# One pair of heads in a fused attention and two-layer network: another order of transposes, scores and products

## The chip, the cores and the metric

The kernel runs on one core of one Trainium2 chip. The metric is the device time of one execution in microseconds (us), as the median of several runs. An engine takes its instructions strictly in the order in which the program lists them; the engines meet only where one waits for a result of another. The names are those of the profile: PE is the matrix engine (PEld its weight loads), DVE the vector engine, ACT the scalar engine, SP the engine that issues most transfers.

## The reference

```python
scores = scale * np.matmul(q, k.transpose(0, 1, 3, 2))      # 2 batches, 12 heads, 448 x 64
scores = np.where(mask, -1000000000.0, scores)              # causal
scores = scores - np.max(scores, axis=-1, keepdims=True)
attn = np.exp(scores)
attn = attn / (np.sum(attn, axis=-1, keepdims=True) + 1e-09)
x = np.matmul(attn, v)                                      # then (896, 768)
h = np.maximum(x @ w_in, 0.0);  x = h * h @ w_out           # d_ff = 2048
h = x @ w_in2;                  out = (h - np.tanh(h)) @ w_out2
```

## The kernel before, in words

Two heads make a pair; there are twelve pairs, six for each batch (`NPAIR`, line 28). The 448 queries of a head are seven chunks of 64, and since the mask is causal chunk c needs keys 0 to 64(c+1)-1. A pair's work is cut into parts, each a function of `body`:

- `scores(n, t)` (lines 262 to 284), PE: the scores of half t of the pair's chunks, in two banks of PSUM. Half 0 is chunks 6, 5 and 0, half 1 is chunks 3, 2, 4 and 1 (`STEPS`, line 51; the first pair swaps them). Two small matmuls per bank add the mask (line 281). The banks of tag "s" are four, so a half's banks are those of the same half of the pair before.
- `maxes(n, t)` (lines 286 to 294), DVE: one maximum per chunk (line 292), and one scaling of the row of maxima (line 294).
- `exps(n, t, z)` (line 301), ACT: the exponentials with their sums.
- `recips(n)` (lines 305, 306), DVE: one over the sums. `norms(n, cs)` (line 313), DVE: the division, one instruction per chunk, in place, of 64(c+1) columns.
- `transposes(n, t)` (lines 315 to 322), PE: four of the sixteen 128x128 blocks of the probabilities into one bank of tag "t" (two such banks), and then on ACT the copy out to SBUF (line 322). Block group 0 reads chunks 0 to 3, group 1 chunks 4, 5, 6 and 2, groups 2 and 3 chunks 3 to 6.
- `pv(n, kcs)` (line 334), PE: the products with V, for key blocks 0 to 3. Key block 0 needs the copies of groups 0 and 1, block 1 that of group 2, blocks 2 and 3 that of group 3.
- `xhi` and `xlo` (lines 347, 351): the pair's output as a rounded high part (ACT) and a remainder (DVE).

The loop of lines 463 to 503 runs over s, and works on three pairs at once: the scores of pair s, the softmax of pair p = s-1, and transposes and products of pair a = s-2. No scheduler moves anything: an engine's queue is the order in which the loop's calls list its instructions.

Beside it the loop prepares the weights of the network. `one()` (lines 168 to 172) takes one DVE step of that list (`shift`, `merge`, `sign`, `split`, lines 113 to 134) if the step's budget allows, which is about one step per pair. The ACT work that belongs to it (lines 103 and 125) is kept in `act_late` and issued where `late()` (line 164) is called.

After the loop, lines 505 to 538 finish the last two pairs between the first matmul groups of the network (`first`, line 422, `group`, lines 357 to 367), and lines 540 to 555 run the network. Its matmuls have the lines 364, 365 and 366.

Of the kernel before, what the change touches and what calls it, by code (L numbers as in the profile page):

```python
# [8 lines left out]
F32 = mybir.dt.float32  # L9
# [13 lines left out]
P = 128  # L23
# [39 lines left out]
def body(ctx: ExitStack, tc: tile.TileContext, qT, kT, vL, w1, w2, w3, w4, out):  # L63
    nc = tc.nc
    sb = ctx.enter_context(tc.tile_pool(name="sb", bufs=1))
    ps = ctx.enter_context(tc.tile_pool(name="ps", bufs=1, space=PSUM))
# [7 lines left out]
    def slot(i, shape, dt, name):  # L74
        return sb.tile(shape, dt, tag=f"slot{i}", name=name)
# [75 lines left out]
    def room():  # L151
        i = len(taken) - RING
        return i < 0 or taken[i] < freed[0]
# [10 lines left out]
    def late():  # L164
        while act_late:
            act_late.pop(0)()

    def one():

        if todo and budget[0] > 0 and (room() or not todo[0][3]):  # L170
            take()
            return True

    def take():
        f, cost, _, _ = todo.pop(0)
        f()
        budget[0] -= cost
# [19 lines left out]
    def load_qk(n):  # L197
        if n < NPAIR:
            b, hp = divmod(n, NP)
            qk[n] = (tmp(f"q{n}"), tmp(f"k{n}", "w"))  # L200
            nc.sync.dma_start(out=qk[n][0], in_=qT[b, hp])
            (nc.scalar if n == 0 else nc.sync).dma_start(out=qk[n][1], in_=kT[b, hp])

    def load_v(b):
        t = sb.tile([P, 3, DM], F32, tag=f"v{b}", name=f"v{b}")
        nc.sync.dma_start(out=t, in_=vL[b, : 3 * P].rearrange("(t p) d -> p t d", p=P))
        if b == 0:
            vs["end"] = slot(7, [D, B, DM], F32, "vend")
            nc.sync.dma_start(out=vs["end"], in_=vL[:, 3 * P :].rearrange("b p d -> p b d"))
        vs[b] = [t[:, 0], t[:, 1], t[:, 2], vs["end"][:, b]]  # L210
# [5 lines left out]
    def warm(count):  # L216
        o = ps.tile([P, 512], F32, tag="o", bufs=2, name="warm")[:, :S]
        for _ in range(count):
            nc.tensor.matmul(o, lhsT=ones[:, :P], rhs=ones, start=True, stop=True)  # L219
# [33 lines left out]
    sc = {}  # L253
    stat = {}
    pt = {}
    ob = {}

    def step(n, t):

        return STEPS[1 - t if n == 0 else t]  # L260

    def scores(n, t):
        q, k = qk[n]
        banks = []
        for z, cs in enumerate(step(n, t)):
            bank = ps.tile([P, 512], F32, tag="s", bufs=4, name=f"s{n}_{t}_{z}")
            banks.append(bank)
            for c in cs:
                sc[n, c] = bank[:, SOFF[c] : SOFF[c] + D * (c + 1)]
        for i in range(2):  # L270
            for z, cs in enumerate(step(n, t)):
                for c in cs[i : i + 1]:
                    for j in range(2):
                        r, e = slice(D * j, D * j + D), D * (j ^ z)
                        nc.tensor.matmul(sc[n, c][e : e + D], lhsT=q[r, D * c : D * c + D], rhs=k[r, : D * (c + 1)], start=(c == cs[0]), stop=False, skip_group_check=True)  # L275
        for z, cs in enumerate(step(n, t)):
            d = [SOFF[c] // D + c for c in cs]
            o = banks[z].rearrange("p (b k) -> p b k", k=D)[:, d[0] : d[-1] + 1 : max(d[-1] - d[0], 1)]
            for j in range(2):
                r, e = slice(D * j, D * j + D), D * (j ^ z)  # L280
                nc.tensor.matmul(o[e : e + D], lhsT=identb[r, r], rhs=maskb[r, : len(cs)], start=False, stop=True, skip_group_check=True)
        if t == 1:
            qk.pop(n)
            load_qk(n + 3)

    def maxes(n, t):
        if t == 0:
            stat[n] = sb.tile([P, 3, 8], F32, tag="stat", bufs=3, name=f"st{n}")
        st = stat[n]
        cs = [c for b in step(n, t) for c in b]  # L290
        for c in cs:
            nc.vector.tensor_reduce(out=st[:, 0, SI[c] : SI[c] + 1], in_=sc[n, c], axis=AX.X, op=ALU.max, negate=True)  # L292
        a, z = SI[cs[0]], SI[cs[-1]] + 1
        nc.vector.tensor_scalar_mul(out=st[:, 0, a:z], in0=st[:, 0, a:z], scalar1=0.125)  # L294

    def exps(n, t, z):
        st = stat[n]
        for c in step(n, t)[z]:
            w = D * (c + 1)
            i = SI[c]  # L300
            nc.scalar.activation(prob[n % 3][:, POFF[c] : POFF[c] + w], sc.pop((n, c)), AF.Exp, bias=st[:, 0, i : i + 1], scale=0.125, accum_out=st[:, 1, i : i + 1])  # L301

    def recips(n):
        st = stat[n]
        nc.vector.tensor_scalar_add(out=st[:, 1, :NQ], in0=st[:, 1, :NQ], scalar1=1e-9)
        nc.vector.reciprocal(out=st[:, 2, :NQ], in_=st[:, 1, :NQ])

    def norms(n, cs):
        st = stat[n]
        for c in cs:  # L310
            i = SI[c]
            p = prob[n % 3][:, POFF[c] : POFF[c] + D * (c + 1)]
            nc.vector.tensor_scalar_mul(out=p, in0=p, scalar1=st[:, 2, i : i + 1])  # L313

    def transposes(n, t):
        if t == 0:
            pt[n] = slot(3 + n % 2, [P, 16, P], F32, f"pt{n}")
        bank = ps.tile([P, 512], F32, tag="t", bufs=2, name=f"t{n}_{t}")
        for i, (kc, c) in enumerate(TBLK[4 * t : 4 * t + 4]):
            o = bank.rearrange("p (i j q) -> p i j q", j=2, q=D)[:, i, :: -1 if c in TURNED else 1]  # L320
            nc.tensor.transpose(o, prob[n % 3][:, POFF[c] + P * kc : POFF[c] + P * kc + P], ident)  # L321
        nc.scalar.copy(out=pt[n][:, 4 * t : 4 * t + 4], in_=bank.rearrange("p (i q) -> p i q", q=P))  # L322

    def pv(n, kcs):
        b, hp = divmod(n, NP)
        if 0 in kcs:
            ob[n] = ps.tile([P, 512], F32, tag="o", bufs=2, name=f"o{n}")
        o = ob[n]
        for kc in kcs:
            r = P if kc < 3 else D  # L330
            m = NQ - 2 * kc
            for j in range(2):
                h = 2 * hp + j
                nc.tensor.matmul(  # L334
                    o[D * j : D * j + D, P * kc : S],
                    lhsT=vs[b][kc][:r, D * h : D * h + D],
                    rhs=pt[n][:r, TBASE[kc] : TBASE[kc] + m, D * j : D * j + D],
                    start=(kc == 0),
                    stop=(kc == 3),
                    skip_group_check=True,  # L340
                )
        if 3 in kcs:
            pt.pop(n)

    def xhi(n):
        b, hp = divmod(n, NP)
        nc.scalar.copy(out=x[hp][:, 0, b], in_=ob[n][:, :S])  # L347

    def xlo(n):
        b, hp = divmod(n, NP)  # L350
        nc.vector.tensor_sub(out=x[hp][:, 1, b], in0=ob.pop(n)[:, :S], in1=x[hp][:, 0, b])
# [111 lines left out]
    for s in range(NPAIR):  # L463
        p, a = s - 1, s - 2
        sp, sa = p >= 0, a >= 0
        budget[0] = min(budget[0], 0) + (SHARE_PAIR if s > 1 else 0)
        if sa:
            transposes(a, 0)
        if sp:
            maxes(p, 1)  # L470
            exps(p, 1, 0)
        if sa:
            transposes(a, 1)
        if sp:
            exps(p, 1, 1)
        one()
        if a >= 1:
            xhi(a - 1)
        scores(s, 0)
        maxes(s, 0)  # L480
        if sp:
            recips(p)
            norms(p, (3, 2))
        if s == 2:
            warm(5)
        if a >= 1:
            xlo(a - 1)
        if sa:
            transposes(a, 2)
            transposes(a, 3)  # L490
        exps(s, 0, 0)
        exps(s, 0, 1)
        if sp:
            norms(p, (1, 0, 4, 5, 6))
        if sa:
            pv(a, (0, 1))
        late()
        scores(s, 1)
        one()
        if sa:  # L500
            pv(a, (2, 3))
        if s == 1:
            load_v(1)

    p, a = NPAIR - 1, NPAIR - 2
    budget[0] = min(budget[0], 0) + SHARE_LAST
    transposes(a, 0)
    maxes(p, 1)
    exps(p, 1, 0)
    transposes(a, 1)  # L510
    exps(p, 1, 1)
    one()
    xhi(a - 1)
    act = first(0, 0, 0, 0)
    recips(p)
    norms(p, (3, 2))
    xlo(a - 1)
    transposes(a, 2)
    transposes(a, 3)
    act()  # L520
    norms(p, (1, 0, 4, 5, 6))
    act = first(0, 0, 1, 0)
    pv(a, range(4))
    late()
# [5 lines left out]
    act = first(0, 0, 2, 0)  # L530
    for t in range(4):
        transposes(p, t)
    act()
    pv(p, range(4))
    late()
# [57 lines left out]
```

## Time and profile before

| | |
|---|---|
| median of 3 runs | 568.91 us (567.93 to 569.95) |
| profiled execution, its own time | 567.94 us |
| span of the profiled execution | 566.2 us |
| PE busy | 553.8 us, 98% of the span |
| DVE busy | 405.6 us, 72% |
| ACT busy | 336.8 us, 59% |
| PE, DVE, ACT busy from 37.04 to 78.53 us (six pairs) | 39.68, 38.26, 36.47 of 41.49 us |
| first matmul of the network (line 364) | 85.25 us after the span's start |

The span goes from the first to the last instruction; the execution's own time has 1.7 us more around it. The shares of the whole span are means over two stages: some 85 us of attention, in which three engines hand work to each other, and 480 us of network, in which PE works without a break.

### The profile page before, as it was taken

To read this page: it belongs to the slowest core of one execution; us is meant where nothing else is said; L and a number is where in the kernel's file an instruction comes from. 1 tells how busy PE (TensorE), PEld (TensorE's weight loads), DVE (VectorE), ACT (ScalarE), POOL (GpSimd) and SP (SyncE) were. 2 spreads that over 40 slices of the span, in tenths; PEclk is the share of its full clock that TensorE was granted. 3 is DMA by queue.
4 is the path that set the end of the run, shared out by engine and by line. 5 is a ranking of instruction groups with operands and counts; after the bars stand their busy time and mean duration, and the time that the engine had idled before them with its cause. 6 is when DMAs were issued, how large, how long until landed. Compare 5 with 4: busy or idle time off the path is not lost.

```text
span 566.2 us, 8063 instructions
## 1 busy us (share of the span) xinstructions
PE 553.8 (98%) x3134; PEld 479.5 (85%) x3134; DVE 405.6 (72%) x727; ACT 336.8 (59%) x650; POOL 1.8 (0%) x11
## 2 busy tenths in 40 slices
PE   6899999999999999999999999999999999999997
PEld 3455558899999999999999999999999999999996
DVE  5889995588667527665648579998887499898511
ACT  4798896777654336666424258786565487864100
POOL 1000000000000000000000000000000000000000
PEclk9999999999999999999999999999999999999999
DMA  8732301245355514333133330110665311015211
GB/s 279 296 123 66 107 1 57 59 164 167 113 168 167 168 56 168 111 112 111 57 112 112 111 113 1 56 56 11 214 218 172 118 50 56 1 57 184 81 49 49
DMA packets 15525, 61.85 MB, mean 109 GB/s; under 512 B 1664, under 2 KB 6400, under 8 KB 15488
## 3 DMA queue, kind: packets, MB, share of 16 engines
q1 hardware_dynamic: 15200, 61.00, 32.5%
q8 instruction: 24, 0.39, 0.3%
q10 hardware_dynamic: 288, 0.34, 0.2%
q14 instruction: 13, 0.11, 0.1%
HBM read 58.59 MB, written 2.75 MB: 108 GB/s over the span
## 4 chain that ended last, share of the span: by engine, by line
PE 90%; ACT 8%; DVE 2%; issue 0%; DVEq 0%; ACTq 0%
PE o L364 14%; PE o L365 14%; PE h L364 14%; PE o L366 14%; PE h L366 14%; PE h L365 14%; ACT p L301 4%; ACT pt L322 3%; PE o L334 3%; PE s L275 2%; PE t L321 1%; DVE st L292 1%; PE warm L219 1%; ACT x L347 1%; DVE p L313 0%
## 5 line engine op out<-in xcount | busy, mean ns | idle before, releaser
L364 PE MATMUL o<-g,w 128*128 128x448 f32 x384 | 141.3, 368 | 0.0
L365 PE MATMUL o<-g,w 128*128 128x448 f32 x384 | 141.2, 368 | 0.0
L366 PE MATMUL o<-g,w 128*128 128x448 f32 x384 | 140.3, 365 | 0.0
L364 PEld LDWEIGHTS o<-g,w 128*128 128x128 f32 x384 | 71.9, 187 | 7.2
L366 PEld LDWEIGHTS o<-g,w 128*128 128x128 f32 x384 | 72.1, 188 | 6.9
L125 ACT CAST w<-raw 128x768 fp32r<-128x768 f32 x64 | 57.9, 904 | 33.3 <-DVE raw L123 33.2
L365 PEld LDWEIGHTS o<-g,w 128*128 128x128 f32 x384 | 72.1, 188 | 6.4
L103 ACT ACTIVATE raw<-raw 128x768 f32<-128x768 f32 x64 | 59.3, 926 | 23.9 <-DMA raw<-w 23.9
L364 PE MATMUL h<-y,w 128*128 128x448 f32 x192 | 70.5, 367 | 0.0
L364 PE MATMUL h<-x,w 128*128 128x448 f32 x192 | 70.4, 367 | 0.0
L366 PE MATMUL h<-x,w 128*128 128x448 f32 x192 | 70.0, 365 | 0.0
L366 PE MATMUL h<-y,w 128*128 128x448 f32 x192 | 69.7, 363 | 0.0
L365 PE MATMUL h<-x,w 128*128 128x448 f32 x192 | 69.5, 362 | 0.0
L365 PE MATMUL h<-y,w 128*128 128x448 f32 x192 | 69.3, 361 | 0.0
L123 DVE SCALAR_TENSOR_TENSOR raw<-raw 128x768 int32<-128x768 int32 x64 | 61.2, 956 | 1.3
L118 DVE SCALAR_TENSOR_TENSOR raw<-raw 128x768 int32<-128x768 int32 x64 | 61.0, 953 | 0.9 <-ACT raw L103 0.9
L134 DVE TENSOR_TENSOR w<-raw,w 128x768 fp32r<-128x768 f32 x32 | 30.6, 958 | 28.0 <-ACT w L125 27.9
L373 DVE TENSOR_TENSOR g<-r,g 128x448 fp32r<-128x448 f32 x32 | 20.0, 625 | 37.8 <-ACT g L370 37.8
L301 ACT ACTIVATE p<-s,st 128x256 f32<-128x256 f32 (+6 forms) x84 | 40.1, 511 | 8.1 <-DVE st L294 7.0
L132 DVE SCALAR_TENSOR_TENSOR w<-w,raw 128x768 fp32r<-128x768 f32 x32 | 30.7, 959 | 18.7 <-ACT w L125 18.5
L366 PEld LDWEIGHTS h<-y,w 128*128 128x128 f32 x192 | 35.9, 187 | 3.5
L366 PEld LDWEIGHTS h<-x,w 128*128 128x128 f32 x192 | 36.0, 187 | 3.0
(57 smaller groups left out, 742.7 us busy)
## 6 DMA issues: line engine op xcount, KB each, us to landing
raw<-w SPq DMA_DIRECT2D x64, 768.0 KB, 4.3
q<-qT SPq DMA_DIRECT2D x12, 224.0 KB, 4.6
k<-kT SPq DMA_DIRECT2D x11, 224.0 KB, 3.1
out<-part SPq DMA_DIRECT2D x11, 224.0 KB, 1.9
v<-vL SPq DMA_DIRECT2D x2, 1152.0 KB, 10.1
vend<-vL SPq DMA_DIRECT2D x1, 384.0 KB, 10.0
k<-kT ACTq DMA_DIRECT2D x1, 224.0 KB, 3.5
out<-part ACTq DMA_DIRECT2D x1, 112.0 KB, 1.7
```

The costliest lines, as they stand in the source:

```text
L103: nc.scalar.activation(h, h, AF.Copy, scale=2.0**-112)
L118: nc.vector.scalar_tensor_tensor(out=lo, in0=hi, scalar=3, in1=lo, op0=ALU.logical_shift_left, op1=ALU.bitwise_or)
L123: nc.vector.scalar_tensor_tensor(out=lo, in0=hi, scalar=-0x80000000, in1=lo, op0=ALU.bitwise_and, op1=ALU.bitwise_or)
L125: act_late.append(lambda: nc.scalar.copy(out=st["w"][:, 0], in_=lo.bitcast(F32)))
L132: nc.vector.scalar_tensor_tensor(out=w[:, 1], in0=w[:, 0].bitcast(F32), scalar=-(1.0 - 2.0**-24), in1=f, op0=ALU.mult, op1=ALU.add)
L134: nc.vector.tensor_sub(out=w[:, 1], in0=f, in1=w[:, 0])
L301: nc.scalar.activation(prob[n % 3][:, POFF[c] : POFF[c] + w], sc.pop((n, c)), AF.Exp, bias=st[:, 0, i : i + 1], scale=0.125, accum_out=st[ ...
L322: nc.scalar.copy(out=pt[n][:, 4 * t : 4 * t + 4], in_=bank.rearrange("p (i q) -> p i q", q=P))
L364: nc.tensor.matmul(h, lhsT=hi, rhs=xh, start=(k == 0), stop=False)
L365: nc.tensor.matmul(h, lhsT=hi, rhs=xl, start=False, stop=False)
L366: nc.tensor.matmul(h, lhsT=lo, rhs=xh, start=False, stop=(k == kk - 1))
L373: nc.vector.tensor_sub(out=dst[1], in0=v, in1=dst[0])
```

## The change

The copies leave `transposes` and become a function of their own, `tcopy`. Within a step the order becomes: transposes of groups 0 and 1, scores of half 0, transposes of groups 2 and 3, scores of half 1, and then all products with V in one run. On ACT both exponentials of half 1 come first and the copies of groups 0 and 1 behind them, and `late()` stands ahead of the exponentials of half 0. On DVE the divisions are cut elsewhere: chunks 1, 0, 2 and 3 stay in the step of the sums, chunks 4, 5 and 6 go to the next step, behind the maxima of half 1. No instruction is added or left out.

```diff
--- before.py
+++ after.py
@@ -253,6 +253,7 @@
     sc = {}
     stat = {}
     pt = {}
+    tb = {}
     ob = {}
 
     def step(n, t):
@@ -313,12 +314,15 @@
             nc.vector.tensor_scalar_mul(out=p, in0=p, scalar1=st[:, 2, i : i + 1])
 
     def transposes(n, t):
-        if t == 0:
-            pt[n] = slot(3 + n % 2, [P, 16, P], F32, f"pt{n}")
-        bank = ps.tile([P, 512], F32, tag="t", bufs=2, name=f"t{n}_{t}")
+        bank = tb[n, t] = ps.tile([P, 512], F32, tag="t", bufs=2, name=f"t{n}_{t}")
         for i, (kc, c) in enumerate(TBLK[4 * t : 4 * t + 4]):
             o = bank.rearrange("p (i j q) -> p i j q", j=2, q=D)[:, i, :: -1 if c in TURNED else 1]
             nc.tensor.transpose(o, prob[n % 3][:, POFF[c] + P * kc : POFF[c] + P * kc + P], ident)
+
+    def tcopy(n, t):
+        if t == 0:
+            pt[n] = slot(3 + n % 2, [P, 16, P], F32, f"pt{n}")
+        bank = tb.pop((n, t))
         nc.scalar.copy(out=pt[n][:, 4 * t : 4 * t + 4], in_=bank.rearrange("p (i q) -> p i q", q=P))
 
     def pv(n, kcs):
@@ -464,61 +468,67 @@
         p, a = s - 1, s - 2
         sp, sa = p >= 0, a >= 0
         budget[0] = min(budget[0], 0) + (SHARE_PAIR if s > 1 else 0)
-        if sa:
-            transposes(a, 0)
         if sp:
             maxes(p, 1)
-            exps(p, 1, 0)
         if sa:
+            norms(a, (4, 5, 6))
+            transposes(a, 0)
             transposes(a, 1)
         if sp:
+            exps(p, 1, 0)
             exps(p, 1, 1)
+        if sa:
+            tcopy(a, 0)
+            tcopy(a, 1)
         one()
         if a >= 1:
             xhi(a - 1)
         scores(s, 0)
         maxes(s, 0)
+        if s == 2:
+            warm(5)
         if sp:
             recips(p)
-            norms(p, (3, 2))
-        if s == 2:
-            warm(5)
+        if sa:
+            transposes(a, 2)
+            tcopy(a, 2)
+            transposes(a, 3)
+            tcopy(a, 3)
+        if sp:
+            norms(p, (1, 0, 2, 3))
+        late()
+        exps(s, 0, 0)
+        exps(s, 0, 1)
         if a >= 1:
             xlo(a - 1)
+        one()
+        scores(s, 1)
         if sa:
-            transposes(a, 2)
-            transposes(a, 3)
-        exps(s, 0, 0)
-        exps(s, 0, 1)
-        if sp:
-            norms(p, (1, 0, 4, 5, 6))
-        if sa:
-            pv(a, (0, 1))
-        late()
-        scores(s, 1)
-        one()
-        if sa:
-            pv(a, (2, 3))
+            pv(a, range(4))
         if s == 1:
             load_v(1)
 
     p, a = NPAIR - 1, NPAIR - 2
     budget[0] = min(budget[0], 0) + SHARE_LAST
+    maxes(p, 1)
+    norms(a, (4, 5, 6))
     transposes(a, 0)
-    maxes(p, 1)
+    transposes(a, 1)
     exps(p, 1, 0)
-    transposes(a, 1)
     exps(p, 1, 1)
+    tcopy(a, 0)
+    tcopy(a, 1)
     one()
     xhi(a - 1)
     act = first(0, 0, 0, 0)
     recips(p)
-    norms(p, (3, 2))
     xlo(a - 1)
     transposes(a, 2)
+    tcopy(a, 2)
     transposes(a, 3)
+    tcopy(a, 3)
     act()
-    norms(p, (1, 0, 4, 5, 6))
+    norms(p, (1, 0, 2, 3, 4, 5, 6))
     act = first(0, 0, 1, 0)
     pv(a, range(4))
     late()
@@ -530,6 +540,7 @@
     act = first(0, 0, 2, 0)
     for t in range(4):
         transposes(p, t)
+        tcopy(p, t)
     act()
     pv(p, range(4))
     late()
```

DVE, in step 4 of the loop and into step 5; s is a bank of scores, st the row of statistics of a pair, p the probabilities of a pair, x its output, o its products. Before:

```order
L351 TENSOR_TENSOR x_68<-o_403,x_68 128x448 [waits Activation_49]
L313 TENSOR_SCALAR p_126<-p_126,st_373 128x128
L313 TENSOR_SCALAR p_126<-p_126,st_373 128x64
L313 TENSOR_SCALAR p_126<-p_126,st_373 128x320
L313 TENSOR_SCALAR p_126<-p_126,st_373 128x384
L313 TENSOR_SCALAR p_126<-p_126,st_373 128x448
L292 TENSOR_REDUCE st_468<-s_1_0_503 128x1 [waits PE_49]
L292 TENSOR_REDUCE st_468<-s_1_0_503 128x1
L292 TENSOR_REDUCE st_468<-s_1_1_504 128x1 [waits PE_49]
L292 TENSOR_REDUCE st_468<-s_1_1_504 128x1
L294 TENSOR_SCALAR st_468<-st_468 128x4 [waits DVE_49]
L134 TENSOR_TENSOR w_359<-raw_120,w_359 128x768
```

The same place now (line numbers are higher by one to four):

```order
L314 TENSOR_SCALAR p_126<-p_126,st_373 128x192
L314 TENSOR_SCALAR p_126<-p_126,st_373 128x256
L355 TENSOR_TENSOR x_68<-o_420,x_68 128x448 [waits Activation_49]
L293 TENSOR_REDUCE st_468<-s_1_0_495 128x1 [waits PE_49]
L293 TENSOR_REDUCE st_468<-s_1_0_495 128x1
L293 TENSOR_REDUCE st_468<-s_1_1_496 128x1 [waits PE_49]
L293 TENSOR_REDUCE st_468<-s_1_1_496 128x1
L295 TENSOR_SCALAR st_468<-st_468 128x4 [waits DVE_49]
L314 TENSOR_SCALAR p_126<-p_126,st_373 128x320
L314 TENSOR_SCALAR p_126<-p_126,st_373 128x384
L314 TENSOR_SCALAR p_126<-p_126,st_373 128x448
L134 TENSOR_TENSOR w_359<-raw_120,w_359 128x768
```

The divisions of 320, 384 and 448 columns of a pair stood ahead of the maxima of the other pair's half 1; now they stand behind these maxima and their scaling, and ahead of the step of weight preparation.

PE, the end of step 4; t is a bank of transposes, pt their copies, v the values. Before:

```order
L334 MATMUL o_498<-pt_432,v_112 64x448 x2
L334 MATMUL o_498<-pt_432,v_112 64x320 [waits Activation_49]
L334 MATMUL o_498<-pt_432,v_112 64x320
L275 MATMUL s_1_0_503<-k_232,q_231 64x256 x2
L275 MATMUL s_1_1_504<-k_232,q_231 64x320 x2
L275 MATMUL s_1_0_503<-k_232,q_231 64x192 x2
L275 MATMUL s_1_1_504<-k_232,q_231 64x128 x2
L281 LDWEIGHTS identb
L281 MATMUL s_1_0_503<-maskb,identb 64x2x64
L281 LDWEIGHTS identb
L281 MATMUL s_1_0_503<-maskb,identb 64x2x64
```

Now:

```order
L282 LDWEIGHTS identb
L282 MATMUL s_1_1_496<-maskb,identb 64x2x64
L282 LDWEIGHTS identb
L282 MATMUL s_1_1_496<-maskb,identb 64x2x64
L338 MATMUL o_513<-pt_451,v_112 64x448 x2
L338 MATMUL o_513<-pt_451,v_112 64x320 [waits Activation_49]
L338 MATMUL o_513<-pt_451,v_112 64x320
L338 MATMUL o_513<-pt_451,v_112 64x192 [waits Activation_49]
L338 MATMUL o_513<-pt_451,v_112 64x192
L338 MATMUL o_513<-pt_451,vend 64x64 x2
L320 MATMUL t_0_530<-ident,p_126 128x2x64 [waits DVE_49,PE_49]
```

The scores of half 1 stood between the products of key blocks 1 and 2, and so behind two waits for copies; now all products stand behind these scores, and ahead of the next transposes.

ACT, step 5. Before:

```order
L301 ACTIVATE p_127,st_468<-s_0_0_456,st_468 128x448 [waits DVE_49]
L301 ACTIVATE p_127,st_468<-s_0_1_457,st_468 128x384
L301 ACTIVATE p_127,st_468<-s_0_1_457,st_468 128x64
L322 COPY pt_525<-t_0_526 128x512 [waits PE_49,Activation_49]
L301 ACTIVATE p_127,st_468<-s_1_0_503,st_468 128x256 [waits DVE_49]
L301 ACTIVATE p_127,st_468<-s_1_0_503,st_468 128x192
L322 COPY pt_525<-t_1_539 128x512 [waits PE_49]
L301 ACTIVATE p_127,st_468<-s_1_1_504,st_468 128x320
L301 ACTIVATE p_127,st_468<-s_1_1_504,st_468 128x128
L347 CAST x_69<-o_498 128x448
L322 COPY pt_525<-t_2_573 128x512 [waits PE_49]
L322 COPY pt_525<-t_3_579 128x512 [waits PE_49]
```

Now:

```order
L302 ACTIVATE p_127,st_468<-s_0_0_456,st_468 128x448 [waits DVE_49]
L302 ACTIVATE p_127,st_468<-s_0_1_457,st_468 128x384
L302 ACTIVATE p_127,st_468<-s_0_1_457,st_468 128x64
L302 ACTIVATE p_127,st_468<-s_1_0_495,st_468 128x256 [waits DVE_49,PE_49]
L302 ACTIVATE p_127,st_468<-s_1_0_495,st_468 128x192
L302 ACTIVATE p_127,st_468<-s_1_1_496,st_468 128x320 [waits PE_49]
L302 ACTIVATE p_127,st_468<-s_1_1_496,st_468 128x128
L326 COPY pt_544<-t_0_530 128x512 [waits PE_49,Activation_49]
L326 COPY pt_544<-t_1_535 128x512 [waits PE_49]
L351 CAST x_69<-o_513 128x448
L326 COPY pt_544<-t_2_570 128x512 [waits PE_49]
L326 COPY pt_544<-t_3_576 128x512 [waits PE_49]
```

The copies of groups 0 and 1 stood ahead of and between the exponentials of half 1 (256, 192, 320 and 128 columns), and now stand behind all four.

## Rows read from the trace of the kernel before

**Rows 1.** One period by stretch: from:to, us, busy PE PEld DVE ACT POOL, clock, DMA.
```profile
50.87:57.79 6.92, 6.62 (x69) 3.77 (x69) 6.44 (x21) 6.47 (x21) 0.00 (x0) 1.00 0.23 66
```
**Rows 2.** Chain that ended last, over one period: start us, us, what.
```profile
43.68 0.59 ACT pt L322
...
47.45 0.76 PE o L334 x4
...
49.92 0.60 PE t L321 x4
...
50.60 0.59 ACT pt L322
```
**Rows 3.** Timeline of DVE, one period: start us, us, engine, line, operation [idle before].
```profile
49.33 1.27 DVE L292 TENSOR_REDUCE st<-s 128x1 f32<-128x256 f32 x4
50.64 0.17 DVE L294 TENSOR_SCALAR st<-st 128x4 f32<-128x4 f32 x1
50.72 0.95 DVE L123 SCALAR_TENSOR_TENSOR raw<-raw 128x768 int32<-128x768 int32 x1
51.97 1.22 DVE L292 TENSOR_REDUCE st<-s 128x1 f32<-128x448 f32 x3 [0.30 <-PE s L281]
53.23 0.17 DVE L294 TENSOR_SCALAR st<-st 128x3 f32<-128x3 f32 x1
53.44 0.17 DVE L305 TENSOR_SCALAR st<-st 128x7 f32<-128x7 f32 x1
53.64 0.20 DVE L306 RECIPROCAL st<-st 128x7 f32<-128x7 f32 x1
53.88 0.58 DVE L313 TENSOR_SCALAR p<-p,st 128x256 f32<-128x256 f32 x2
54.38 0.62 DVE L351 TENSOR_TENSOR x<-o,x 128x448 fp32r<-128x448 f32 x1
54.91 1.43 DVE L313 TENSOR_SCALAR p<-p,st 128x128 f32<-128x128 f32 x5
56.25 0.42 DVE L292 TENSOR_REDUCE st<-s 128x1 f32<-128x256 f32 x1
```
**Rows 4.** Groups by line and form, DVE, 36.98 to 78.5 us: the divisions moved.
```profile
L313 DVE TENSOR_SCALAR p<-p,st 128x448 f32<-128x448 f32 x6 | 2.7, 447 | 0.0
...
L313 DVE TENSOR_SCALAR p<-p,st 128x384 f32<-128x384 f32 x6 | 2.5, 413 | 0.0
L313 DVE TENSOR_SCALAR p<-p,st 128x320 f32<-128x320 f32 x6 | 2.3, 379 | 0.0
```
**Rows 5.** Timelines of DVE, PEld and PE: where scores wait for divisions, and maxima for scores.
```profile
11.86 1.93 DVE L313 TENSOR_SCALAR p<-p,st 128x256 f32<-128x256 f32 x7
...
13.84 0.20 PEld L321 LDWEIGHTS t<-ident,p 128*128 128x128 f32 x2 [0.23 <-DVE p L313]
14.21 0.21 PEld L275 LDWEIGHTS s<-k,q 64*64 64x64 f32 x8 [0.17 <-ACT pt L322]
...
50.87 0.99 PE L275 MATMUL s<-k,q 64*64 64x448 f32 x12
```
**Rows 6.** Timelines of PEld, ACT and DVE in the step of pair 2.
```profile
15.19 0.69 PEld L219 LDWEIGHTS <-const-bfloat16-1.0 128*128 128x128 bf16 x5
...
17.40 1.09 ACT L322 COPY pt<-t 128x512 f32<-128x512 f32 x2
...
19.81 0.96 ACT L103 ACTIVATE raw<-raw 128x768 f32<-128x768 f32 x1
...
20.80 0.96 DVE L118 SCALAR_TENSOR_TENSOR raw<-raw 128x768 int32<-128x768 int32 x1 [0.86 <-ACT raw L103]
21.68 0.42 DVE L292 TENSOR_REDUCE st<-s 128x1 f32<-128x256 f32 x1
```
**Rows 7.** Timeline of PEld at the end of attention: last transposes, first matmul of the network.
```profile
84.42 0.86 PEld L321 LDWEIGHTS t<-ident,p 128*128 128x128 f32 x8
85.25 0.19 PEld L364 LDWEIGHTS h<-x,w 128*128 128x128 f32 x1
```

## The prediction

> **What bounds the kernel now.** I read the views in this order: busy time by stretch, the chain that ended last, then the timelines of single engines. From the first matmul of the network on, at 85.25 us [rows 7], PE works without a break and the change touches nothing, so what counts is by how much that matmul moves. It stands at the end of a regular stretch: one pair every 6.92 us, at a granted clock of 1.00, which is the 2.4 GHz level, with PE busy for 6.62 of it, DVE for 6.44 and ACT for 6.47 [rows 1]. In that table the reader is to see that three engines are nearly full, so none has much to give. The chain over one period says what closes the loop today: it runs through copies and exponentials on ACT, then through products, scores and transposes on PE, and back to the next copy 6.92 us later [rows 2]. DVE is not on it, but waits only 0.30 us for scores in each period [rows 3].
>
> The change takes PE out of ACT's way: the products no longer wait for the copies of groups 2 and 3 ahead of the scores of half 1. The question is which loop is the longest after it. The new order on DVE makes one: transposes of group 1 read chunks 4, 5 and 6; the divisions of these now stand behind the maxima of half 1 of the next pair; the scores of half 0 stand on PE behind those transposes; and the maxima of half 0 wait on DVE for these scores. DVE does nothing else in that wait but one step of weight preparation.
>
> **The loop through DVE, link by link.** I start the count at the first maximum of half 1 and use distances from start to start.
>
> 1. Four maxima: 49.33 to 50.64, 1.31. Their scaling: the next independent instruction starts 0.08 later [rows 3].
> 2. Divisions of chunks 4, 5 and 6: 0.379, 0.413 and 0.447 long [rows 4]. Five such divisions run from 54.91 to 56.34, while the next instruction starts at 56.25 [rows 3], so neighbours overlap by 0.09; I take 0.08. The three end 0.30 + 0.33 + 0.447 = 1.08 after the first starts.
> 3. Seven divisions end at 13.79 and the transposes that waited for them start at 13.84: 0.05. Those are the last two of group 1, just the two that will stand behind chunk 6's division, and the scores start at 14.21: 0.37 [rows 5].
> 4. Scores start at 50.87 [rows 5], the maxima of half 0, which waited for them, at 51.97: 1.10 [rows 3].
> 5. Maxima of half 0: 51.97 to 53.23, 1.26. Scaling 0.08, as in link 1. The sums are ready by then (ACT's exponentials of half 1 start right after link 1), so today's longer gap to 53.44 goes. One over the sums: 53.44 to 53.64 to 53.88, 0.44 [rows 3].
> 6. Divisions of chunks 1, 0, 2 and 3: all seven take 53.88 to 54.38 and 54.91 to 56.25, 1.84 [rows 3]; less 0.30 + 0.33 + 0.36 for the three of link 2 leaves 0.85. Then the remainder of the output, 54.38 to 54.91: 0.53. Then the next maxima.
>
> Links 1 to 3 are 1.31 + 0.08 + 1.08 + 0.05 + 0.37 = 2.89; the whole loop is 2.89 + 1.10 + 1.26 + 0.08 + 0.44 + 0.85 + 0.53 = **7.15 us, against 6.92 now**: 0.23 more for each pair. Between divisions and maxima of half 0, DVE has 3.99 - 2.38 = 1.61 us, of which the weight step takes 0.95 [rows 3]; some 0.66 us are a wait that takes the place of 0.30 today.
>
> The other engines fit into 7.15. PE's 6.62 hold waits that now fall away, and ACT's 6.47 contain a weight step [rows 1]. On PE the scores of half 1 follow about 2 us after those of half 0 and so are there more than 1 us before DVE comes to them; the products stand in the time in which PE would wait for the divisions anyway. On ACT the copies wait for nothing that is late. `late()`, now ahead of the exponentials of half 0, puts one weight step ahead of them; they are not needed before the sums of the next step. SP issues the same transfers in the same order, each behind the scores it followed before. So what the change saves on PE (a run of products without a change of kind in its middle, no wait for copies) is covered by the wait for DVE, and costs or gives nothing.
>
> **The start.** The divisions of pair 0 begin at 11.86 as now [rows 5]. Four of them (0.85) instead of seven stand ahead of the maxima of pair 1's half 1, which start at 12.71. By links 1 to 3 the scores of pair 2 start at 15.60 (14.21 now [rows 5]), and by links 4 to 6 DVE is through with the divisions of pair 1 at 15.60 + 1.10 + 1.26 + 0.08 + 0.44 + 0.85 = 19.33. In this step a second weight step follows (line 118), which waits for ACT's line 103. ACT does it behind the copies of groups 2 and 3: scores about 0.97, five warming matmuls about 0.75 [rows 6], transposes and 0.70 to the copy (49.92 to 50.60 in the chain [rows 2]), two copies with 0.94 to the next instruction (1.09 long [rows 6], less an overlap of 0.15 as among ACT's neighbours), so it starts at 18.96, ends 0.96 later [rows 6], and line 118 starts at 19.95 and holds DVE for 0.88 (20.80 to 21.68 [rows 6]). The maxima of pair 2's half 1 start at about 20.83.
>
> **The sum.** Nine loops of 7.15 us bring the maxima of pair 11's half 1 to 20.83 + 64.35 = 85.18. The network's first matmul takes the place of the next scores: 2.89 later, less 0.17, because the eight transposes ahead of it take 0.83 to its start [rows 7] and there is no gap of 0.17 as there is to the scores [rows 5]. That is 87.90, against 85.25: **+2.65 us**. The profiled execution would go from 567.94 to 570.6 us. It lies 0.97 us under the median of the runs, 568.91; I forecast for the median: **571.6 us**. The tail behind it keeps its length, since PE is full there and the copies of pairs 10 and 11 have a whole matmul group of the network to land in.
>
> Bounds: a hundredth of a microsecond in the loop is a tenth in the sum. Links 3 and 4 are each one crossing of engines, read from one or two places; 0.06 either way is 0.6 us. The start is between 20.21 for the maxima (line 118 waits for nothing: 19.33 + 0.88) and 21.5 (a copy or a transfer late): -0.6 to +0.7. Together +1.3 to +4.0 us.
>
> A page to weigh against link 2: five divisions that sum to more than 1.7 us start and hand over within 1.34 [rows 3], so neighbours on DVE overlap. The Trainium skill, VectorE: DVE Perf Modes, section The DRAIN you can't avoid, says that the next operation does not start until the pipe is empty, though one that is not held starts earlier. With full durations everywhere the loop would come to some 8 us and the sum to over 10 us more; the trace decides for the overlap.
>
> **Rivals.**
>
> *Faster: DVE's loop does not close.* Were the three divisions done before PE reaches group 1, DVE would run through without the wait and need its busy 6.44 us [rows 1] for a pair: 9 x 0.71 = 6.4 us less than in my sum, that is -3.7 us, 565.2 us. It decides if the maxima of half 1 start at least 0.66 us earlier in the loop than I have them. For it speaks that PE offers these scores over 1 us early; against it, that DVE's queue is in order and the loop needs nothing else to be late. 0.07.
>
> *No change: links shorter, start as early as it can be.* A loop of 7.00 to 7.05 us and a start at 20.2 give +0.7 to +1.1 us, 569.6 to 570.0 us. For it speaks that 0.23 us per pair is little; against it, that each link is read from this trace. 0.14.
>
> *Slower by more: ACT.* Where two ACT weight steps fall on one pair, both now stand ahead of the exponentials of half 0: 0.96 each on top of an ACT that is busy for 6.47 with one [rows 1], together above 7.15. The excess of 0.2 to 0.3 us would reach DVE in a few pairs: 572.5 us. For it speaks the sum, against it that such pairs are few. 0.05.
>
> *Slower: the clock.* PE's wait in a pair becomes one of about a microsecond, in three pieces, where today's clock stays at 1.00 through all of them [rows 1]. If it fell to the 1.2 GHz level for a pair, PE's some 6.2 us of work would double and cost about 5 us: 576 us. The Trainium skill, TensorE: Matmul & The Clock Gate, section A second HAM failure mode: psum-queue depth-cycling, describes a matrix engine that goes idle for moments between groups often enough to swing between the two levels. By that rule today's waits should show it, and the trace does not agree. 0.03.
>
> That the change is not what it says I exclude: the order shows the moves on all three engines.
>
> **How the numbers follow.** The forecast has 0.71, with its own range of 570.2 to 572.9 us. About 0.3% (1.7 us, so 567.2 and 570.6) is what a measurement of this kernel can tell from no change. Of the forecast's 0.71 some 0.10 lies below 570.6; with the second rival's 0.14 that is 0.24, of which I give 0.02 to the other two signs: 0.22 for no change. Faster: 0.08. Slower: 0.70. The range of 569.3 to 573.3 holds the forecast, most of the second rival and the third.
>
> **What would show it.** Right, step by step: a period of 7.1 to 7.2 us; DVE's idle time before line 293 at 0.6 to 0.7 per pair, ended by scores; PE's weight loads of the transposes (line 320) waiting for line 314, three times a pair; products without a wait for copies; the chain that ended last running through DVE instead of ACT; the network's first matmul near 87.9 us; clock 1.00. Wrong: a period under 6.9 us, transposes that wait for copies and not for divisions, or a chain that still runs through ACT.

## The result, and the profile after

The changed kernel takes **572.77 us** (median of 4 runs, 572.37 to 572.93), the kernel before 568.77 us in the same session: a ratio of 1.0071, with a 95% interval of 1.0056 to 1.0087. It is slower by about 4.0 us, inside the stated range, and 1.2 us more than forecast. The profiled execution has a span of 570.6 us against 566.2. All of these 4.4 us lie ahead of the network: its first matmul starts at 89.66 us instead of 85.25 [rows 7].

| | before | after |
|---|---|---|
| median | 568.77 us | 572.77 us |
| span of the profiled execution | 566.2 us | 570.6 us |
| first matmul of the network | 85.25 us | 89.66 us |
| a pair's period in the regular stretch | 6.92 us | 7.14 us |
| scores of pair 3 start | 21.48 us | 25.58 us |

The chain that ended last, over one period of the changed kernel (start us, us, what), answers to [rows 2]:

```profile
51.35 1.20 DVE st L293 x4
...
52.74 0.30 DVE p L314
...
53.18 0.57 PE t L320 x2
...
53.78 0.44 PE t L320 x2
54.22 0.92 PE s L276 x8
55.13 0.13 PE s L282 x4
55.26 1.21 DVE st L293 x3
...
57.02 0.94 DVE p L314 x4
57.96 0.53 DVE x L355
58.49 1.20 DVE st L293 x4
```

Before, it ran through copies and exponentials on ACT; in this period ACT is not in it now. It goes from the maxima of half 1 to the divisions of chunks 4 to 6, to the transposes of group 1 and the scores on PE, and back to the maxima on DVE: 51.35 to 58.49, 7.14 us. The timeline of DVE in the same period answers to [rows 3]:

```profile
51.26 1.27 DVE L293 TENSOR_REDUCE st<-s 128x1 f32<-128x256 f32 x4
52.57 0.17 DVE L295 TENSOR_SCALAR st<-st 128x4 f32<-128x4 f32 x1
52.65 1.07 DVE L314 TENSOR_SCALAR p<-p,st 128x320 f32<-128x320 f32 x3
53.64 0.95 DVE L123 SCALAR_TENSOR_TENSOR raw<-raw 128x768 int32<-128x768 int32 x1
55.25 1.22 DVE L293 TENSOR_REDUCE st<-s 128x1 f32<-128x448 f32 x3 [0.66 <-PE s L282]
...
58.41 1.27 DVE L293 TENSOR_REDUCE st<-s 128x1 f32<-128x256 f32 x4
```

The wait for scores has grown from 0.30 to 0.66 us. Busy time by stretch over this period (PE, PEld, DVE, ACT, POOL, then granted clock, DMA) answers to [rows 1]; no engine is busy all through:

```profile
51.26:58.41 7.15, 6.72 (x72) 4.00 (x70) 6.36 (x22) 6.53 (x23) 0.00 (x0) 1.00 0.22 67
```

What the forecast did not have is in the same view of the start:

```profile
12.00:14.00 2.00, 0.73 (x4) 0.45 (x4) 1.97 (x9) 1.42 (x6) 0.00 (x0) 1.00 1.07 426
14.00:16.00 2.00, 1.20 (x4) 0.57 (x4) 1.84 (x7) 1.49 (x7) 0.00 (x0) 0.84 1.00 409
16.00:18.00 2.00, 2.00 (x18) 0.98 (x18) 0.04 (x1) 1.30 (x4) 0.00 (x0) 0.50 1.01 410
18.00:20.00 2.00, 2.00 (x12) 1.29 (x12) 1.90 (x8) 0.10 (x1) 0.00 (x0) 0.81 1.03 378
```

The granted clock, in the last column but two, falls to 0.50, the 1.2 GHz level, from some point in 14 to 16 us until some point in 18 to 20 us. Two rows of PE's timeline tell what came before and what it cost:

```profile
14.76 1.38 PE L320 MATMUL t<-ident,p 128*128 128x128 f32 x4 [1.36 <-DVE p L314]
16.08 1.77 PE L276 MATMUL s<-k,q 64*64 64x448 f32 x12
```

PE had waited 1.36 us for the divisions of pair 0 that now stand behind the maxima of pair 1, and the scores of pair 2 then take 1.77 us instead of the 0.99 of the same instructions at the full level [rows 5]. In the kernel before, the clock is 1.00 over these microseconds.

### The profile page after: what moved, and what is told of

It is laid out like the page before. It is cut to its first block, busy times and chain, and to the rows that moved or that the text cites. A ratio compares the mean times of both kernels' runs of the same rounds, so it can differ in the third digit from the quotient of the medians.

```text
span 570.6 us, 8074 instructions
## 1 busy us (share of the span) xinstructions
PE 557.2 (98%) x3134; PEld 482.4 (85%) x3134; DVE 404.7 (71%) x727; ACT 337.4 (59%) x650; POOL 1.8 (0%) x11
## 4 chain that ended last, share of the span: by engine, by line
PE 89%; DVE 9%; ACT 1%; issue 1%; DVEq 0%; ACTq 0%
PE o L368 14%; PE o L369 14%; PE h L368 14%; PE o L370 14%; PE h L370 14%; PE h L369 13%; DVE st L293 5%; PE t L320 3%; PE s L276 2%; DVE p L314 2%; PE warm L219 1%; DVE x L355 1%; PE o L338 1%; DVE st L295 1%; DVE st L307 0%
## 5 line engine op out<-in xcount | busy, mean ns | idle before, releaser
L320 PE MATMUL t<-ident,p 128*128 128x128 f32 x192 | 33.2, 291 | 7.2 <-DVE p L314 6.5
L293 DVE TENSOR_REDUCE st<-s 128x1 f32<-128x256 f32 (+6 forms) x84 | 30.0, 416 | 12.6 <-PE s L282 12.6
```

## The experiments

Theory: the loop through DVE sets the period, and the clock's fall makes the start longer. The rivals are under each run. Ratios are against the kernel before on the same chip, with their 95% intervals.

| kernel | time, us | ratio | period, us | first matmul of the network, us | clock, 14 to 20 us |
|---|---|---|---|---|---|
| changed kernel, again | 572.92 | 1.0072 (1.0047 to 1.0098) | 7.14 | 90.38 | 0.50 |
| warming in the gap | 570.88 | 1.0044 (1.0030 to 1.0057) | 7.14 | 88.46 | 1.00 |
| divisions in one run | 570.37 | 1.0034 (1.0021 to 1.0046) | 7.14, alternating | 87.78 | 1.00 |
| before, divisions cut | 578.30 | 1.0159 (1.0138 to 1.0181) | 7.43 | 95.61 | 0.73 |
| products split | 576.41 | 1.0142 (1.0128 to 1.0156) | 7.55 | 93.72 | 0.72 |
| divisions cut, copies old | 572.65 | 1.0068 (1.0042 to 1.0094) | 7.14 | 90.47 | 0.51 |
| divisions in one run, copies old | 565.27 | 0.9939 (0.9916 to 0.9963) | 6.68 | 82.39 | 1.00 |
| the same, weight steps old | 566.53 | 0.9967 (0.9956 to 0.9977) | 6.69 | 83.81 | 1.00 |
| divisions in one run, copies first | 564.10 | 0.9919 (0.9892 to 0.9945) | 6.59 | 81.32 | 1.00 |

**The clock at the start.** Five warming matmuls are added where PE waits, between the transposes of groups 0 and 1 (the expectations count the groups from 1):

```diff
             transposes(a, 0)
+            if s == 2:
+                warm(5)
             transposes(a, 1)
```

> The changed kernel with five warming matmuls put between transposes 1 and 2 of the third step, where PE waits 1.36 us for divisions and after which its granted clock was 0.50 (16 to 18 us). Theory (loop through DVE at 7.14 us a pair, and besides a start made longer by the fall of the clock): clock 1.00 from 14 to 20 us, the scores of pair 2 take 0.99 us instead of 1.77, the first matmul of the network comes about 1.6 us earlier (88.0 instead of 89.66), the period stays at 7.14; 571.2 us instead of 572.8. Rival (the clock's fall is covered by a wait for a transfer or for ACT in that step): clock back, time unchanged at 572.8 us.

The clock stays at 1.00 and the period at 7.14. By the two ratios (1.0071 and 1.0044, whose intervals just touch) this is worth 0.27% or 1.5 us, as expected. The network's first matmul comes at 88.46 and not at 88.0, because this profile's first maximum was 0.3 us later than the changed kernel's (6.10 against 5.80; its first scores began only 0.06 us later, but took 1.60 us instead of 1.37, and why is open). Counted from the first maximum, that matmul comes 82.36 us on, against 83.86 in the changed kernel: 1.50 us earlier, the same as by the ratios. So the fall costs time, and the rival that it is covered falls.

The changed kernel, run again, shows the fall again, and longer (0.50 over all of 14 to 20 us and 0.81 from 20 to 22, where some 3 us were expected). The network's first matmul is 84.88 us behind the first maximum here, 1.0 us more than in the shorter fall:

> The changed kernel once more, on the same chip as the three others, as their measure: 572 to 573 us, period 7.14 us, granted clock at the 1.2 GHz level for some 3 us around 17 us, in this profile too if the fall belongs to the order of work and not to chance.

**The divisions alone put back.** The three lines of the change that cut them are undone (the third, a `norms` behind the loop, is left out here):

```diff
-            norms(a, (4, 5, 6))
             transposes(a, 0)
...
-            norms(p, (1, 0, 2, 3))
+            norms(p, (1, 0, 2, 3, 4, 5, 6))
```

> The changed kernel with all seven divisions of a pair in one run, ahead of the next pair's maxima, as before; the order of PE and ACT stays that of the change. Theory (the loop is made by the divisions of chunks 4 to 6 behind the maxima): that loop is open, DVE works without a wait and its own 6.49 us a pair are the period (6.5 to 6.6); no long wait of PE at the start, clock 1.00 there; the network's first matmul near 81 to 83 us; 564 to 566.5 us, faster than both kernels. Rival (the new order on PE and ACT, copies behind the exponentials and products behind all scores, is what costs): the period stays above 6.92 us and the time at 569 us or more.

This is where the theory missed by 4 us. The clock stays at 1.00 and in the regular stretch PE no longer waits for divisions, but two pairs still take 14.28 us (50.40 to 64.68, first maxima of half 1). The rival's bound, a period above 6.92 and 569 us or more, holds. The chain that ended last shows a second loop, over two pairs:

```profile
50.49 1.20 DVE st L293 x4
...
52.35 1.46 ACT p L302 x7
53.81 0.48 ACT pt L326
...
54.34 1.14 PE t L320 x8
55.48 0.92 PE s L276 x16
...
56.46 2.03 PE o L338 x16
58.48 1.02 PE t L320 x8
59.51 0.92 PE s L276 x8
...
60.55 1.21 DVE st L293 x3
...
62.30 1.93 DVE p L314 x7
64.23 0.53 DVE x L355
64.76 1.20 DVE st L293 x4
```

Maxima of half 1 release the exponentials; the copy of group 0 now stands behind all four of these; the transposes of group 2 need the bank that this copy empties; scores of half 1, then all products, then the next transposes and scores stand behind on PE; and DVE waits for these scores. So the change closes a second loop, and to open the first alone frees nothing of the period.

That both give 7.14 us a pair is chance. All seven divisions stand in the second loop here (1.93 us); in the changed kernel only four do (0.94, at 57.02 above), so there it is about 1 us shorter: an estimate of 13.3 us for two pairs, against the 14.28 that the loop through DVE needs for them. PE shows the same margin. Its transposes of groups 0 and 1 take 1.02 us here (58.48 above); in the changed kernel, with the waits for divisions between them, it is 2.02 us from the first of them to the scores:

```profile
59.27 0.42 PEld L320 LDWEIGHTS t<-ident,p 128*128 128x128 f32 x4
...
61.29 0.21 PEld L276 LDWEIGHTS s<-k,q 64*64 64x64 f32 x8 [0.17 <-issue]
```

Putting the divisions back opened the first loop and lengthened the second.

**One part of the change alone.** The kernel before, with only the divisions cut:

```diff
             maxes(p, 1)
+            if sa:
+                norms(a, (4, 5, 6))
             exps(p, 1, 0)
...
-            norms(p, (1, 0, 4, 5, 6))
+            norms(p, (1, 0))
```

> The kernel before with one part of the change alone: divisions of chunks 4, 5 and 6 behind the maxima of the next pair's half 1; PE's and ACT's order as before. Theory: this alone closes the loop through DVE, at least 7.14 us a pair, and a little more because copies and exponentials of ACT alternate and the copy of group 1 now waits for late transposes ahead of the second half of the exponentials: 7.2 to 7.5 us, 572 to 576 us. Rival (the split is harmless, PE's and ACT's order is the loss): period 6.92, 568.8 us.

The period is 7.43, as expected, but not for the reason given. The cut alone makes a loop, and a longer one than in the change; what lengthens it is not ACT. In this stretch the chain that ended last has only DVE and PE, and the products of key blocks 0 and 1 stand in it, ahead of the scores of half 1:

```profile
51.37 0.92 PE s L275 x8
...
52.34 1.02 PE t L321 x8
53.37 1.44 PE o L334 x8
54.81 0.92 PE s L275 x16
...
55.86 1.28 DVE st L292 x4
```

So DVE waits a second time in each period, for the scores of half 1 (the row at 63.27):

```profile
59.83 1.22 DVE L292 TENSOR_REDUCE st<-s 128x1 f32<-128x448 f32 x3 [0.65 <-PE s L281]
...
63.27 1.28 DVE L292 TENSOR_REDUCE st<-s 128x1 f32<-128x256 f32 x4 [0.20 <-PE s L281]
...
67.26 1.22 DVE L292 TENSOR_REDUCE st<-s 128x1 f32<-128x448 f32 x3 [1.05 <-PE s L281]
```

The time lies 2.3 us above the range, which had nothing for the clock. In the profile it fell twice, in 16 to 20 us and again in 26 to 32 us (0.50 over 28 to 30), where the maxima of half 1 of two successive pairs are 8.83 us apart (24.72 to 33.55) instead of 7.43. The five timed runs fall into two groups: two of 575.9 us with a mean clock of 0.997, inside the range, and three of 578.3 to 578.7 with 0.991 to 0.994.

**The products.** In the changed kernel they go back to both sides of the scores:

```diff
+        if sa:
+            pv(a, (0, 1))
         one()
         scores(s, 1)
         if sa:
-            pv(a, range(4))
+            pv(a, (2, 3))
```

> The changed kernel with the products of key blocks 0 and 1 again ahead of the scores of half 1, and 2 and 3 behind; all else as changed. Theory (the products in one run are a gain, hidden under the loop through DVE, where scores of half 1 are ready 1.1 us before DVE takes them): the scores of half 1 come 1.44 us later on PE, 0.4 us after DVE is ready for them, so the loop grows to about 7.5 us, 575 to 577 us. Rival (the place of the products does not matter in either order): 572.8 us, period 7.14.

576.41 us and 7.55 us: as expected. DVE now waits 0.32 us for the scores of half 1 too. The products in one run behind the scores are thus a gain: where they stand decides whether the scores of half 1 come in time for DVE.

**The second loop.** If there are two, the copies alone put back must change nothing, and both parts put back must free the gain. The edit to ACT's order is the same in both runs:

```diff
             transposes(a, 0)
+            tcopy(a, 0)
             transposes(a, 1)
         if sp:
             exps(p, 1, 0)
+        if sa:
+            tcopy(a, 1)
+        if sp:
             exps(p, 1, 1)
-        if sa:
-            tcopy(a, 0)
-            tcopy(a, 1)
```

With the divisions still cut:

> The changed kernel with ACT's copies of groups 0 and 1 back at their places before; the divisions stay cut. Theory of two loops: the one through DVE stays as it is, 7.14 us a pair, 572 to 573.5 us. Rival (the copies behind the exponentials make the change's loss, the cut divisions only look like it): period under 7.0 us, 570 us or less.

572.65 us, period 7.14: the loop through DVE stands by itself. With the divisions in one run as well (the expectation takes both loops to be equally long in the change itself; by the estimate above the second is shorter there):

> PE's order of the change (products in one run), but all seven divisions in one run and ACT's copies of groups 0 and 1 where they were before (ahead of and between the exponentials of half 1). New theory, after the divisions in one run alone gave 570.4 us: the change makes two loops of nearly the same length, one through the divided divisions (7.14 us) and one through the copies behind the exponentials, which keep transposes 2 and 3 and with them scores, products and the next scores waiting (14.25 us for two pairs); only both undone free the gain of the products in one run. Then the period is 6.6 to 6.8 us and the time 566 to 567.5 us, under the kernel before. Rival (the products in one run are themselves the loss): period 6.9 us or more, 568.5 us or more.

565.27 us, 0.7 us better than the range: 6.68 us a pair. This run and the one before differ in the divisions alone and ran on one chip: the cut costs 7.4 us here, of it 0.46 us a pair in the regular stretch. The rival that PE's order is the loss falls. The chain has left DVE; in part of this stretch it reads:

```profile
46.22 2.03 PE o L338 x16
48.25 0.60 PE t L320 x4
...
48.93 0.58 ACT pt L326
49.51 0.97 ACT p L302 x4
50.48 0.47 ACT pt L326
50.95 0.87 ACT p L302 x4
```

That kernel also keeps a small move of the change, ACT's weight steps ahead of the exponentials of half 0. Put back (`late()` behind `exps(s, 0, 1)`):

> The run with divisions in one run and copies at their old places (565.3 us), with ACT's weight steps behind the exponentials of half 0 again, as in the kernel before. It tells how much of that run's gain of 2.7 us over the kernel before is the order of PE and how much is the place of the weight steps. If PE's order is all of it: 565.3 us, no change. If the two weight steps of the fourth step, which in the kernel before made one interval between scores 8.4 us long, are a part: that interval grows again, the period of 6.7 us stays, 566 to 566.8 us.

566.53 us: by the ratios 0.28% or 1.6 us of the 0.61% belong to that move, the rest, 0.33%, to PE's order and the smaller edits left in. The intervals of the two runs overlap a little, so the first share is less sure than the second, whose interval is clear of 1. The place was not the one named: scores in the fourth step are 7.20 us apart, but those of the third step 8.16 (14.71 to 22.87), where DVE waits for ACT's weight step, line 103; without the edit it is 7.38 (14.24 to 21.62). The network's first matmuls of the two profiles are 1.42 us apart: 0.78 of it comes from this step, 0.18 from the fourth, and 0.47 was there before either, at the first maximum (6.09 against 5.62).

**A version that beats both.** Both copies ahead of both exponentials, divisions in one run, products in one run:

```diff
             transposes(a, 0)
+            tcopy(a, 0)
             transposes(a, 1)
+            tcopy(a, 1)
         if sp:
             exps(p, 1, 0)
             exps(p, 1, 1)
-        if sa:
-            tcopy(a, 0)
-            tcopy(a, 1)
```

> As the run with the divisions in one run and the copies at their old places, but both copies of groups 0 and 1 ahead of both exponentials of half 1. Theory of two loops: transposes 3 no longer wait for a copy that stands between exponentials, DVE's 6.49 us of work and ACT's 6.47 are what is left: period 6.5 to 6.6 us, 564 to 566 us, the fastest of all. Rival (exponentials that start later delay the sums and through them DVE): period 6.8 us or more, 567 us or more.

564.10 us and 6.59 us a pair, 0.8% under the kernel before. The numbers are as expected, but what is left is neither DVE nor ACT: it is PE. Its chain in the regular stretch has PE alone, and busy time by stretch says the same, PE 26.00 of 26.00:

```profile
45.60 2.03 PE o L338 x16
47.63 1.02 PE t L320 x8
48.65 0.92 PE s L276 x8
...
49.63 1.02 PE t L320 x8
50.66 1.11 PE s L276 x9
...
52.19 2.03 PE o L338 x16
```

```profile
43.00:69.00 26.00, 26.00 (x266) 16.08 (x268) 24.95 (x81) 24.02 (x78) 0.00 (x0) 1.00 0.24 77
```

## Why the prediction was right, and where it was not

- *The loop through DVE, link by link: right.* 7.15 us forecast, 7.14 measured; the wait of DVE 0.66 in both. Links 3 and 4, from divisions to scores and from scores to maxima, were each read from one place of the trace before, and held (0.42 and 1.10 in both). The transposes of group 1 wait for line 314 as foretold, and the chain runs through DVE instead of ACT. All nine periods are 7.14 or 7.15 us, so the rival of two ACT weight steps on one pair shows nowhere.
- *Nine such loops and the tail: right.* From the maxima of pair 2's half 1 (22.69) to the network's first matmul (89.66) it is 66.97 us, against 67.07 forecast. The spans differ by 4.4 us, as that matmul does (89.66 - 85.25): nothing was lost or won behind it.
- *The start: mis-sized.* Maxima of pair 2's half 1 were to start at 20.83; they start at 22.69 in the profile after, 1.86 later, of which 0.21 is this profile's later first maximum (5.80 against 5.59). The scores of pair 2 and five warming matmuls were costed at the full clock. With PE warmed in the gap, the network's first matmul comes 82.36 us after the first maximum (88.46 - 6.10); the forecast had 82.31 (87.90 - 5.59). So the error of the sum is the clock, some 1.5 us by the timed runs; with the warming the change costs 0.44%, 2.5 us, where 2.65 were forecast. By its own terms the lower bound is +1.45 rather than +1.3; nothing hangs on it.
- *The rival "Slower: the clock": its place was wrong.* I looked for it in the regular stretch, with 5 us a pair and a chance of 0.03, and took the trace of the kernel before, whose waits lowered no clock, as the evidence. It came once, at the start, where two waits of PE now stand close together, and cost less. Nor is the kernel before free of it: six of its 36 timed runs beside the experiments list a mean clock of 0.994 to 0.997, and they are its longest (569.36 to 571.84 us). The Trainium skill, TensorE: Matmul & The Clock Gate, section A second HAM failure mode: psum-queue depth-cycling, speaks of a matrix engine that goes idle for moments between groups and swings between the levels. At the start the trace shows one such swing (0.50 in 16 to 18 us); in the regular stretch, with three waits a pair of 0.16 to 0.61 us, it shows none (1.00).
- *"On ACT the copies wait for nothing that is late": true, but it left out a wait.* The copies are late themselves, behind all four exponentials, and PE stands behind them: in the regular stretch its weight loads wait 0.16 to 0.20 us for one in each period. That is part of the second loop. It did not change the time here, because in the changed kernel that loop is the shorter one, by some 1 us in two pairs by the estimate above. It did spoil what I expected of the divisions put back, where it grows to 14.28 us.
- *"What the change saves on PE is covered": right for the sum, too simple as a reason.* The period came out at 7.14 with nothing counted for PE, and where both loops are open, PE's order is part of a gain of 0.33%. But the place of the products does count in the changed kernel: split again, they lose 0.71% or 4.0 us more (1.0142 less 1.0071), because the scores of half 1 then come too late.
- *The rival "Faster": its price was too high.* It took DVE's busy 6.44 us for a pair. With both loops open and the copies first, PE alone needs 6.59.

## What to carry to other kernels

In a software pipeline over engines that each work in order, the period is set by the longest closed loop of waits, which can be longer than the work of the busiest engine: here no engine was busy for more than 6.72 of 7.15 us. Only in the last version was an engine's own work the limit, PE's 6.59 us. Before an order is changed, follow each moved instruction once around to itself in the next round, in every queue that it shares, and add the links; and remember that an experiment that undoes one part also shifts work in the other loops: here the divisions, put back, lengthened the second loop and hid their own gain. Check the first rounds by themselves, since there the waits are others than later.

## What the runs showed of the hardware

The granted clock fell to the 1.2 GHz level in the profile of every kernel with the divisions cut and no warming in the gap (five profiles: 0.50 to 0.73 over 14 to 20 us), and in no other profile. The timed runs say the same of these orders: all 28 of those five kernels list a mean clock of 0.991 to 0.997, all 31 of the five other kernels made from the change 0.999 or 1.000. The kernel before lies between, with six of 36 at 0.994 to 0.997; no trace shows where in those six it fell.

In the changed kernel PE was busy for 0.73 us of 12 to 14 and 1.20 us of 14 to 16 before the fall, and between two sets of scores, from 11.77 to 16.08 us, it ran nothing but eight transposes. With the divisions in one run PE was busy for 1.05 us of 16 to 18 and 4.65 us of 14 to 20, the same stretch with eight transposes went from 12.29 to 14.95, and the clock stayed at 1.00. What separates the cases was not tried.
